# Two layers of block attention and a gated mixer on one core: preparation of the first row pair, pieces of w_out, weight reloads and the next attention's first units put in other places

## The chip, the core and the metric

The kernel runs on one core of a Trainium2 chip. The core has a matrix engine (PE, with its weight loads PEld), a vector engine (DVE), a scalar engine (ACT), GpSimd (POOL) and SyncE (SP), which here only issues transfers for 16 DMA engines. Each engine works through its own instructions strictly in order; semaphores tie them together. The metric is the device time of one execution in microseconds, lower being better. Before the change it is 2241.38 us, the median of three runs (2240.36 to 2242.91).

## What is computed

Two kinds of layer alternate, A B A B, on one sequence of 2048 rows of 640 elements, with one set of weights for both A and one for both B. Cut from the reference:

```
def _A_ref(x, wq, wk, wv, wo, beta):          # 32 heads of 20, 4 blocks of 512 rows
    q, k, v = (x @ wq), (x @ wk), (x @ wv)    # per head and block
    phi = lambda t: where(t > 0, t + 1.0, exp(t))
    for s in range(4):
        p = softmax(q_s k_s^T * scale + mask); a_dot = p v_s
        a_mem = (phi(q_s) M) / (phi(q_s) z + 1e-6)
        o = g * a_mem + (1 - g) * a_dot       # g = sigmoid(beta)
        M += phi(k_s)^T v_s; z += sum(phi(k_s))
    return o @ wo

def _B_ref(x, w_in, w_sp, b_sp, w_out):       # 2 * 864 columns
    z = gelu(x @ w_in); z1 = z[:, :864]; z2 = layernorm(z[:, 864:])
    g = w_sp @ z2 + b_sp[:, None]             # over the 2048 rows
    return (z1 * g) @ w_out

x = x + _A_ref(layernorm(x), ...); x = x + _B_ref(layernorm(x), ...)   # twice
```

## The kernel before, in words

Matrices are split into a high and a low half in f16 and multiplied in three products (hh, hl, lh), so a product that looks like 8 matmuls of the sequence is 24 on PE. Rows go in 16 tiles of 128.

The program runs in stages, each over the tiles of one layer: attention of layer 0 (60 to 593 us), the first half of its mixer (`phase1b`, to 795), the fold of its rows with w_sp, the gate and w_out (`phase2f`, to 1151), a lead in which PE already computes the first units of attention 1 (to 1211), attention 1 (to 1695), the mixer of layer 1 (`phase1b` again, to 1897) and its fold (`phase2s`, to the end).

`phase1b` goes over the tiles in the order 0 to 7, 12 to 15, 8 to 11. For each tile PE multiplies the split and transposed activations `th` with w_in in two halves of 30 matmuls (L384). `attn_out` (L352) makes the next tile's attention residual, `xn_t` (L371) its layer norm, its split (`xnhl`) and its transposing DMA into `th` (L309). `z2_half` and `z1_half` read the products out with a gelu. A tile's end is kept in `g.mark[i]`. Inside this stage a list scheduler puts the instructions of each engine in order, the earlier in the program the sooner; `high_priority` and `issue_after` bend that.

`phase2f` folds w_sp over pairs of row tiles, in the manner of Strassen: seven products P1 to P7 of 24 matmuls (L777) for each of eight pairs, over quarters of w_sp that are scaled, split (`hi`, `lo`: L741, L745), turned by a transposing DMA (`T`, L754, into `wt`), stored in `turned` for layer 1 (`st`, L757), copied back to f32 on POOL (`bk`, L762), mixed on DVE (`mS`, L765) and split once more (`H` on ACT, L768; `L` on DVE, L771). P2 needs H1 and L1, P3 H2 and L2. The results are put together on DVE (`v`, `q`, `u`, L784), gated with z1 (`gm`, L829, fetched from DRAM by L788), split (`gh`, `gl`), turned into `ut` (`gT`, L846), multiplied with w_out in a tail of 42 matmuls (`tl`, L854) and added to x (`ad`, L859). `SEVEN` (L695) lists these steps for one pair in the order in which every engine takes them; +n puts a step n pairs later, -n earlier. Steps of the first pair that lie ahead of its P1 form the list `ahead`; the first part of it, up to T12, is put behind the marks of mixer tiles 8 to 15 in equal distances, at high priority. From there on the order is by hand (`manual_schedule`). `staged` (L798) splits w_out into seven pieces (L90 on ACT, L91 on DVE) in `w0`: one behind each product of the first pair. In the last pair w_q, w_k and w_v are loaded back into `zb0`, `zb3` and `zb4` (L958) behind P1, P2 and P3; `turned()` (L1309) brings the normed rows of block 0 as `xt` behind P4 (L1307).

In the lead, `unit` (L1398) makes a tile of 128 columns of q or k for a block of 512 rows in 15 matmuls (L1409). ACT and DVE read it out and split it (L1429, L1433; for k also phi, L1432 to L1450, whose turned form is `pk`, L1452), SP stores it to `st` (L1525, L1526) and later loads it by heads as `qk` (L1539). Units a (q 0), b (k 0) and c (q 1) are written to psum banks of the fold; `kept_back` holds their readouts until the fold's memory is given back. Two tails (`finish`, L973) stand between the units. Then come eight value units (`value`, L1342; 15 matmuls each, L1353), and between them `unit(0, 1, only="k")`, which, called without `own`, makes q and k of tile 1 in new banks, q for the second time.

`phase2s` of layer 1 does the same fold with the quarters stored before: `bring` (L523) loads a stored quarter (L528) or turns one again (L530). `g.wu.load` brings w_out back in 14 loads (L162).

## Time and profile before

| what | value |
|---|---|
| median of three runs | 2241.38 us |
| the profiled execution's own time | 2243.77 us |
| its span, first to last instruction | 2242.0 us |
| mean granted clock of PE | 0.981 |
| attention 0, 60 to 593 us | PE busy 487.09 of 533.00 us, clock 0.97 |
| mixer 0, tiles up to 741.6 us | PE busy 148.12 of 148.60, clock 1.00 |
| fold 0, 854 to 1100 us | PE busy 245.76 of 246.18, DVE 220.59, clock 1.00 |
| attention 1, 1211 to 1695 us | PE busy 456.16 of 483.94, ACT 395.05, POOL 374.81 |
| mixer 1, 1695 to 1897 us | PE busy 201.35 of 202.13 |
| fold 1, from 1921 us | PE busy 315.47 of 321.00, DMA share 0.79 |

The profile is one execution, taken by the hardware profiler, a little slower than the median. The first rows are its whole, the others stretches of it with the busy time of the engines. A row of the timeline gives the start in microseconds, the busy time, the engine, the line, the operation, output and input, the count of equal instructions merged, and in brackets how long the engine had idled before the first of them and what ended that. PE's busy times are modelled from pipelined matmuls, so consecutive rows overlap by some 0.15 us: the distance between two starts is the safer measure. The stretches left out of the table are those that the change touches.

### The profile page before, as it was taken

Reading aid. Unit: us, or ns where it says so; the run is one execution under the profiler, and the core shown is the slowest. Engines: PE = TensorE matmul, PEld = TensorE weight load, DVE = VectorE, ACT = ScalarE, POOL = GpSimd, SP = SyncE. Lnnn points to the kernel's source line nnn. Section 1 sums busy time; section 2 is a strip of 40 time slices with the busy share of each in tenths; the row PEclk is TensorE's granted clock in tenths of the full one; section 3 lists DMA queues with packets and bytes.
Section 4 is the critical chain, followed back from the end, with each engine's and each line's share of the span. In section 5 each row is a group of like instructions: output and inputs, shape, how many; then the busy total and the mean of one; then the engine's idle time right before and its main releaser. Section 6 shows DMA issues by size and latency. Waiting matters only on the chain. (4 is left out here: it accounts for less than half of the span.)

```text
span 2242.0 us, 48924 instructions
## 1 busy us (share of the span) xinstructions
PE 2087.5 (93%) x19740; PEld 1255.8 (56%) x19740; DVE 1623.1 (72%) x2952; ACT 1219.6 (54%) x1491; POOL 1084.2 (48%) x704
## 2 busy tenths in 40 slices
PE   4888999999899888999898999999999999999999
PEld 2455665667555444555454556566665555555555
DVE  8678888787776789899644787877776667465455
ACT  3499888888542333323222898888874334223221
POOL 2398989888332422453330798788884223000000
PEclk9999999999999999999999999999999999999999
DMA  5626535356845667998764345343567334987975
GB/s 163 184 71 216 139 97 141 106 131 178 203 116 185 151 180 189 257 232 231 200 158 136 90 108 133 99 115 103 143 167 206 93 112 129 246 196 189 228 209 133
DMA packets 516340, 356.57 MB, mean 159 GB/s; under 512 B 410064, under 2 KB 452816, under 8 KB 510992
## 3 DMA queue, kind: packets, MB, share of 16 engines
q1 hardware_dynamic: 516112, 353.44, 59.8%
q8 instruction: 155, 2.54, 0.5%
q14 instruction: 73, 0.60, 0.1%
HBM read 157.44 MB, written 107.82 MB: 118 GB/s over the span
## 5 line engine op out<-in xcount | busy, mean ns | idle before, releaser
L1608 POOL TENSOR_TENSOR PHL<-P,PHL 128x1024 f16<-128x1024 f32 x310 | 658.9, 2133 | 204.4 <-ACT PHL L1607 158.2
L1589 ACT ACTIVATE P<-es,sc 128x1024 f32<-128x1024 f32 x320 | 356.2, 1113 | 92.7 <-PE es L1553 90.0
L1599 DVE TENSOR_REDUCE mx<-mp 128x2 f32<-128x1024 f32 (+2 forms) x384 | 321.1, 862 | 85.2 <-PE mp L1553 84.2
L1607 ACT CAST PHL<-P 128x1024 f16<-128x1024 f32 x320 | 333.5, 1042 | 6.3
L384 PEld LDWEIGHTS <-th 128*128 128x128 f16 x1920 | 188.0, 98 | 172.6 <-DMA th<-xnhl 9.6
L777 PEld LDWEIGHTS <-wt 128*128 128x128 f16 x1344 | 132.7, 99 | 142.3 <-DVE wt L771 17.0
L1642 PEld LDWEIGHTS <-PHL 128*128 128x128 f16 x5120 | 167.1, 96 | 56.8 <-DVE oat L1663 19.8
L537 PEld LDWEIGHTS <-wt 128*128 128x128 f16 x1344 | 131.4, 98 | 114.6 <-DMA wt<-wn 2.2
L1642 PE MATMUL pv<-vs,PHL 128*128 128x41 f16 x5120 | 172.7, 181 | 19.7 <-DVE oat L1663 16.5
L384 PE MATMUL zp<-wi,th 128*128 128x432 f16 x960 | 182.1, 348 | 8.0 <-DMA th<-xnhl 7.9
L295 POOL TENSOR_TENSOR lnrs<-lnve,mhalf 128x1 f32<-128x1 f32 x78 | 50.0, 649 | 288.1 <-DVE lnve L294 238.5
L384 PE MATMUL zp<-w,th 128*128 128x432 f16 x960 | 180.4, 346 | 0.7 <-ACT z L397 0.7
L762 POOL TENSOR_TENSOR f<-wt 128x1024 f32<-128x1024 f16 x32 | 82.4, 2577 | 171.1 <-DVE wt L771 124.9
L1409 PEld LDWEIGHTS <-zb 128*128 128x128 f16 x1215 | 105.0, 99 | 105.0 <-issue 9.5
L1582 PEld LDWEIGHTS <-qk 64*128 64x128 f16 (+1 forms) x1728 | 66.0, 94 | 125.6 <-issue 94.5
L1582 PE MATMUL mp<-qk 60*128 60x512 f16 (+3 forms) x864 | 108.5, 305 | 15.1 <-DVE mx L1599 9.7
L1385 PE MATMUL yps<-wo,o 128*128 128x320 f16 x720 | 122.3, 307 | 0.0
L1582 PE MATMUL es<-qk 64*128 64x256 f16 (+3 forms) x864 | 107.0, 300 | 10.1 <-ACT P L1589 7.3
L854 PE MATMUL cyp<-w,ut 128*128 128x320 f16 (+1 forms) x672 | 93.9, 299 | 1.6 <-DMA ut<-un 1.6
L1353 PE MATMUL vps<-zb,zb 128*128 128x320 f16 x480 | 76.8, 309 | 16.9 <-DVE qhl L1433 6.3
L589 DVE SCALAR_TENSOR_TENSOR xo<-cyp,xs,cx 128x640 f32<-128x640 f32 x14 | 12.4, 884 | 107.6 <-DMA out_dram<-xo 80.9
L1353 PE MATMUL vps<-zb,w 128*128 128x320 f16 x480 | 83.6, 306 | 4.4 <-DVE phl L1450 4.4
(299 smaller groups left out, 4238.0 us busy)
## 6 DMA issues: line engine op xcount, KB each, us to landing
wr<-in_B_w_sp_dram SPq DMA_DIRECT2D x32, 1024.0 KB
qk<-st SPq DMA_DIRECT2D x216, 120.0 KB
z<-z SPq DMA_DIRECT2D x32, 432.0 KB
cz<-z SPq DMA_DIRECT2D x32, 432.0 KB
turned<-wt SPq DMA_DIRECT2D x24, 512.0 KB
wt<-turned SPq DMA_DIRECT2D x24, 512.0 KB
st<-qhl SPq DMA_DIRECT2D x41, 256.0 KB
st<-khl SPq DMA_DIRECT2D x40, 256.0 KB
```

The lines of the kernel that those rows point to most:

```text
L384: nc.tensor.matmul(zp[:, n, :FHH], a[:, k, :], b[:, k, c:c + FHH], start=(k == 0 and j == 0), stop=(k == KD - 1 and j == 2))
L537: nc.tensor.matmul(o[:, :FHH], wt[:, x, m, :], zb[b][:, y, m, :], start=start and i == j == 0, stop=i == NP - 1 and j == 2, skip_group_che ...
L777: nc.tensor.matmul(o[:, :FHH], w[:, x, m, :], zb[b][:, y, m, :], start=start and i == j == 0, stop=i == NP - 1 and j == 2, skip_group_chec ...
L1353: nc.tensor.matmul(ps, a[:, k, c], b[:, k, n * 320:(n + 1) * 320], start=(i == 0), stop=(i == 14))
L1385: nc.tensor.matmul(ps, a[:, k, :], b[:, k, c], start=(i == 0), stop=(i == 14))
L1409: nc.tensor.matmul(ps, a[:, k, c], b[:, k, :], start=(i == 0), stop=(i == 14))
L1582: nc.tensor.matmul(out[:, h, o:o + w], a[r, ac], b[r, bc], start=o == 0, stop=False, skip_group_check=True)
L1589: self.last_of["ACT"] = nc.scalar.activation(self.Pf[t], es, AF.Exp, scale=g.esc).ins
L1599: self.last_of["DVE"] = nc.vector.tensor_reduce(mx[:, e, :, i], mp[:, :, o:o + w], AX.X, ALU.max).ins
L1607: nc.scalar.copy(hl[:, 0], P)
L1608: (nc.gpsimd if t < self.T - self.TAIL or t % 2 == 0 else nc.vector).tensor_tensor(hl[:, 1], P, hl[:, 0], ALU.subtract)
L1642: nc.tensor.matmul(pv[:, i, h, 0:PVC - 1], self.P[u][:, x, h, o:o + 128], v[:, j, h0 + h, :], start=first and h == x == 0 and (u, o, i, j) ...
```

## The change

1. `phase1b`: the loads of tile i + 2 are written ahead of tile i's products, and `xn_t` of tile i + 1 directly behind its `attn_out`, both ahead of `z2_half`. This holds for both layers.
2. `phase2f`: the first pair's preparation follows a table, `PREPARED`, which names for each step the mixer tile (1 to 14 in the order of the loop) behind which it stands. Only rows, T and sm or st keep the high priority. Ten steps at the end (H1 to hi22 of the second pair) have no tile and open the order by hand.
3. The pieces of w_out stand behind P1, P3, P4, P5, P6 and P7 of the first pair and P1 and P2 of the second.
4. w_q, w_k and w_v are loaded back behind P4, P5 and P6 of the last pair, `turned()` behind P5. Attention 1's `start` is issued behind the last gate's low half (`nxt.filled`).
5. The lead: three small places of the fold on the right side of memory (`fp`, `ftr1`, `ftr0`) are given back early, and `hl`, `tmp` and `pk` of the units get pools there (`epk`, `eu2`). Nothing is kept back: units a, b, c and d (k 1) are read out as they come, with a tail behind c and a tail behind d. The call in the middle of the values, and with it the second q of tile 1, is gone.

The rows below are orders of instructions as the two kernels have them; the line numbers of the changed kernel are 2 lower in `phase2s` and 5 to 10 higher from `phase2f` on. First SP's queue in the last pair of `phase2f`, before and then changed. The names: `turned` are stores of turned quarters, `zb` the reloaded weights, `cz` and `cx` fetches of z1 and x1, `ut` turned gates, the last transposes those of `turned()`.

```order
L757 DMA turned_1<-wt 128x2048 x2
L958 DMA zb_157<-w_q 128x6400
L788 DMA cz_15376<-z_0_12 128x864
L788 DMA cx_15384<-x_0_13 128x640
L846 DMA_TRANSPOSE ut<-un 128x14x128
L958 DMA zb_158<-w_k 128x6400
L928 DMA x_10<-cx_15267 128x640
L1302 DMA xn<-xnhl 128x1280
L958 DMA zb_159<-w_v 128x6400
L846 DMA_TRANSPOSE ut<-un 128x14x128
L1307 DMA_TRANSPOSE zb_160<-xn 128x10x128 x4
```

The changed kernel's queue from the same place:

```order
L763 DMA turned_1<-wt 128x2048 x2
L794 DMA cz_15375<-z_0_12 128x864
L794 DMA cx_15383<-x_0_13 128x640
L853 DMA_TRANSPOSE ut<-un 128x14x128
L935 DMA x_10<-cx_15267 128x640
L1307 DMA xn<-xnhl 128x1280
L853 DMA_TRANSPOSE ut<-un 128x14x128
L968 DMA zb_157<-w_q 128x6400
L794 DMA cz_15605<-z_0_15 128x864
L968 DMA zb_158<-w_k 128x6400
L1312 DMA_TRANSPOSE zb_160<-xn 128x10x128 x4
```

The fetches of z1 and x1 and both transposes of `ut` moved ahead of the copies; that of w_v comes three rows further down, behind the transposes of `turned()`.

Next DVE in the lead, before: `cx<-cyp` adds a tail's result, `a`, `b`, `c` are the psum banks of the units, `qps` and `kps` those of the second call.

```order
L859 SCALAR_TENSOR_TENSOR cx_15722<-cyp,xs,cx_15722 128x640
L859 SCALAR_TENSOR_TENSOR cx_15759<-cyp,xs,cx_15759 128x640
L1433 SCALAR_TENSOR_TENSOR qhl<-a,qhl 128x512
L1433 SCALAR_TENSOR_TENSOR khl<-b,khl 128x512
L1438 TENSOR_SCALAR b<-b,sc 128x512
L1440 SCALAR_TENSOR_TENSOR b<-eq,sc,b 128x512
L1450 SCALAR_TENSOR_TENSOR phl<-b,sc,phl 128x512
L1433 SCALAR_TENSOR_TENSOR qhl<-c,qhl 128x512
L1359 SCALAR_TENSOR_TENSOR vs<-vps,vs 128x16x20 x2
L1433 SCALAR_TENSOR_TENSOR qhl<-qps,qhl 128x512
L1433 SCALAR_TENSOR_TENSOR khl<-kps,khl 128x512
```

The same stretch of DVE in the changed kernel, up to the values:

```order
L1438 SCALAR_TENSOR_TENSOR qhl<-a,qhl 128x512
L1438 SCALAR_TENSOR_TENSOR khl<-b,khl 128x512
L1443 TENSOR_SCALAR b<-b,sc 128x512
L1445 SCALAR_TENSOR_TENSOR b<-eq,sc,b 128x512
L1455 SCALAR_TENSOR_TENSOR phl<-b,sc,phl 128x512
L1438 SCALAR_TENSOR_TENSOR qhl<-c,qhl 128x512
L866 SCALAR_TENSOR_TENSOR cx_15722<-cyp,xs,cx_15722 128x640
L1438 SCALAR_TENSOR_TENSOR khl<-d,khl 128x512
L1443 TENSOR_SCALAR d<-d,sc 128x512
L1445 SCALAR_TENSOR_TENSOR d<-eq,sc,d 128x512
L1455 SCALAR_TENSOR_TENSOR phl<-d,sc,phl 128x512
L866 SCALAR_TENSOR_TENSOR cx_15759<-cyp,xs,cx_15759 128x640
```

The readouts of a, b and c moved ahead of both additions of the tails; the readout of d replaces that of qps and kps, and the eight readouts of values follow in one piece.

Last SP's queue at the end of layer 1's mixer, before: `th` are turned activations, `x` and `z` loads and stores of the mixer, `wt` the quarters for `phase2s`, `w` pieces of w_out.

```order
L530 DMA_TRANSPOSE wt<-wn 128x16x128
L309 DMA_TRANSPOSE th<-xnhl 128x10x128
L343 DMA x_27398<-x_1_11 128x640
L398 DMA z_1_8<-z_27326 128x864
L309 DMA_TRANSPOSE th<-xnhl 128x10x128
L398 DMA z_1_9<-z_27436 128x864
L309 DMA_TRANSPOSE th<-xnhl 128x10x128
L398 DMA z_1_10<-z_27534 128x864
L528 DMA wt<-turned_1 128x2048
L530 DMA_TRANSPOSE wt<-wn 128x16x128
L162 DMA w_153<-w_uh 128x640
```

And the changed kernel's, from the same activations on:

```order
L309 DMA_TRANSPOSE th<-xnhl 128x10x128
L343 DMA x_27315<-x_1_11 128x640
L398 DMA z_1_8<-z_27312 128x864
L309 DMA_TRANSPOSE th<-xnhl 128x10x128
L398 DMA z_1_9<-z_27422 128x864
L309 DMA_TRANSPOSE th<-xnhl 128x10x128
L398 DMA z_1_10<-z_27520 128x864
L526 DMA wt<-turned_1 128x2048
L526 DMA wt<-turned_0 128x2048
L528 DMA_TRANSPOSE wt<-wn 128x16x128 x2
L398 DMA z_1_11<-z_27613 128x864
L162 DMA w_153<-w_uh 128x640
```

The first transpose of a quarter and the load of a turned quarter, which stood some tiles earlier, moved behind the last but one store of z, next to the other two.

The diff, cut to its core:

```diff
         for i, t in enumerate(ts):
             late = lambda: ExitStack() if i else after(0)
+            b = load(ts[i + 2]) if i + 2 < NT else None
             if i + 1 < NT:
                 with late():
-                    xn = attn_out(ts[i + 1], *a)
+                    th1 = xn_t(attn_out(ts[i + 1], *a))
+            a = b
             last = z2_half(t, w_in_half(1, *th))
             g.mark[i] = last
-            if i + 2 < NT:
-                a = load(ts[i + 2])
-            with late():
-                th1 = xn_t(xn) if i + 1 < NT else None
...
+PREPARED = """
+rows1.0:1 rows0.0:1 max1.0:2 max0.0:4 sm0.0:4 sm1.0:4 hi11.0:5 lo11.0:6 hi22.0:7 lo22.0:8 T11.0:10 T22.0:10 hi21.0:10
+lo21.0:10 bk22.0:10 hi12.0:11 T21.0:11 rows1.1:11 st11.0:11 lo12.0:12 rows0.1:12 bk11.0:12 max1.1:12 st22.0:12 bk21.0:12
+mS1.0:14 mS3.0:14 max0.1:14 H1.0 L1.0 T12.0 mS2.0 sm1.1 sm0.1 hi11.1 st12.0 lo11.1 hi22.1
+""".split()
...
-    def behind(k):
+    def behind(k, n):
         held = ExitStack()
-        held.enter_context(tc.high_priority(offset=HP))
+        if n[0] in "rTs":
+            held.enter_context(tc.high_priority(offset=HP))
...
-    ahead = [(n, w - lag) for w in (-2, -1) for n, lag in order if w - lag >= 0]
-    cut = ahead.index(("T12", 0))
-    for i, (n, k) in enumerate(ahead[:cut]):
-        with behind(min(8 + 8 * i // cut + (n[0] in "Ts"), 15)):
-            item(n, k)
+    ahead = []
+    for w in PREPARED:
+        (n, k), _, m = (w.partition(":")[0].split("."), *w.partition(":")[1:])
+        if m:
+            with behind(int(m), n):
+                item(n, int(k))
+        else:
+            ahead.append((n, int(k)))
...
-            if n[0] == "P" and w == 0:
+            if (w, n) in ((0, "P1"), (0, "P3"), (0, "P4"), (0, "P5"), (0, "P6"), (0, "P7"), (1, "P1"), (1, "P2")):
                 next(wu, None)
-            if w + 1 == NP and n in ("P1", "P2", "P3"):
-                a = "qkv"[int(n[1]) - 1]
+            if w + 1 == NP and n in ("P4", "P5", "P6"):
+                a = "qkv"[int(n[1]) - 4]
                 nc.sync.dma_start(g.wf[a], g.wkept[a])
-            if w + 1 == NP and n == "P4":
-                nxt.turned()
-        if w == 0:
-            for _ in wu:
-                pass
+                if n == "P5":
+                    nxt.turned()
...
     run = lambda it: [None for _ in it]
-    nxt.kept_back = []
-    for nm, m, o in (("q", 0, "a"), ("k", 0, "b"), ("q", 1, "c")):
+    slots.close()
+    nxt.pk = side(nxt.late, "epk", 2)
+    early = ExitStack()
+    nxt.u2 = side(early, "eu2", 3)
+    for nm, m, o in (("q", 0, "a"), ("k", 0, "b"), ("q", 1, "c"), ("k", 1, "d")):
         run(nxt.unit(0, m, {nm: bank(o)}))
-        if (nm, m) != ("q", 0):
+        if m:
             finish(pend.pop(0))
+    early.close()
...
-    todo, nxt.kept_back = nxt.kept_back, None
-    for f_ in todo:
-        f_()
     pb_.close()
     nxt.psum()
     with tc.manual_schedule(engines=ALLE):
         for t in range(4):
             run(nxt.value(t))
-            if t == 0:
-                run(nxt.unit(0, 1, only="k"))
```

24 lines of the change are left out of this document (14 added, 10 removed).

## The prediction, written before the changed kernel was run

> **What bounds the kernel now.** I read the page first, for the engines' shares of the span. Then I read the busy time by stage (the windows view), for the stages in which the busiest engine pauses. Last I read the timeline of each engine there, for what it paused on. In the windows the columns are the stretch, its length, then the busy time and count of PE, of its weight loads, of DVE, ACT and POOL, the granted clock, the DMA share and GB/s.
>
> ```profile
> PE 2087.5 (93%) x19740; PEld 1255.8 (56%) x19740; DVE 1623.1 (72%) x2952; ACT 1219.6 (54%) x1491; POOL 1084.2 (48%) x704
> 741.60:795.06 53.46, 46.05 (x243) 23.83 (x240) 35.98 (x53) 20.04 (x30) 25.40 (x21) 0.97 0.58 153
> 795.06:849.62 54.56, 37.78 (x196) 19.08 (x194) 48.83 (x65) 20.38 (x25) 14.07 (x7) 0.89 0.72 196
> 1100.18:1151.44 51.26, 44.48 (x253) 25.09 (x252) 21.38 (x39) 10.16 (x13) 11.68 (x10) 0.93 0.79 211
> 1151.44:1211.06 59.62, 48.74 (x281) 28.62 (x280) 20.89 (x41) 14.23 (x23) 6.21 (x9) 0.91 0.54 143
> 1897.13:1921.00 23.87, 22.10 (x122) 11.69 (x121) 9.21 (x10) 9.93 (x11) 2.96 (x4) 1.00 1.02 268
> ```
>
> PE sets the time: it is busy for 93% of the span. So a microsecond is won only where PE pauses, or where it does work that goes away. The first four stretches are where this change reaches PE: the last mixer tiles of layer 0, the first pair of its fold, its last pair, and the lead into the second attention. PE idles there for 7.4, 16.8, 6.8 and 10.9 us, 41.9 in all, and the clock is below 1.00 in each. The fifth is the start of layer 1's fold, where PE hardly idles but the DMA engines are full (share 1.02).
>
> **Part 1: the first pair's preparation goes to earlier tiles.** Rows of PE, then of POOL and DVE; the bracket is the idle time ahead and what ended it.
>
> ```profile
> 748.01 5.63 PE L384 MATMUL zp<-w,th 128*128 128x432 f16 x30 [0.71 <-ACT z L397]
> 757.51 7.33 PE L384 MATMUL zp<-wi,th 128*128 128x432 f16 x30 [3.86 <-DMA th<-xnhl]
> 773.15 5.65 PE L384 MATMUL zp<-wi,th 128*128 128x432 f16 x30 [2.83 <-DMA th<-xnhl]
> 743.76 2.12 POOL L762 TENSOR_TENSOR f<-wt 128x1024 f32<-128x1024 f16 x1 [12.14 <-DMA wt<-wn]
> 746.42 0.73 DVE L301 TENSOR_SCALAR z<-z,lnmv,lnrs 128x864 f32<-128x864 f32 x1 [6.68 <-POOL lnrs L295]
> ```
>
> POOL stood 12.14 us at the copy back (L762) of a turned quarter that had not landed. The layer norm's root (L295), queued behind it, came late, DVE waited 6.68 for that, and the split activations reached PE late. In the order of after, T11 and T22 issue some two tiles earlier and POOL's copies come later, when these quarters have landed. So the three waits go: 7.40, and with them 1.69 of low clock (30 matmuls took 7.33 after the 3.86 wait, 5.64 otherwise): 9.1. What is late next: SP now has the store of T11 (st11) ahead of the transposed load th of a following tile, and a store of a quarter can't issue before the quarter has landed. T11 itself issues behind the large stores that keep w_in. The trace shows no such pairing. From below it costs nothing; from above about what went, 9.1. The nearest row is the wait of 3.86, a th held up by the landing of such a quarter, so I take 3.6, one wait of nearly that size without its clock. **Gain 5.5, from 0 to 9.1.**
>
> **Part 2: the fold's first pair and the start of the second.**
>
> ```profile
> 795.06 4.54 PE L777 MATMUL a<-zb,wt 128*128 128x432 f16 x24
> 805.88 0.90 PE L777 MATMUL c<-zb,wt 128*128 128x432 f16 x2 [6.28 <-ACT wt L768]
> 812.61 4.54 PE L777 MATMUL b<-zb,wt 128*128 128x432 f16 x24
> 816.99 4.54 PE L777 MATMUL a<-zb,wt 128*128 128x432 f16 x24
> 841.96 0.53 PE L777 MATMUL c<-zb,wt 128*128 128x432 f16 x2 [2.14 <-DVE u L784]
> 849.62 6.43 PE L777 MATMUL c<-zb,wt 128*128 128x432 f16 x22 [7.13 <-DVE wt L771]
> ```
>
> A product of 24 matmuls takes 4.38 from start to start (812.61 to 816.99). The second product waited 6.28 for H1, which now is made before the mixer ends; so is L1. Three products then take 13.1, not the 21.9 from 795.06 to 816.99. But the gain does not reach the end of the second pair's start whole. That pair's second product needs L1 of its own rows. The chain to it starts with a transposed quarter that reuses a tile of the first pair and waits for the third product to end; before, 32.6 passed from there to the product's resumption at 849.62. DVE is busy for 48.83 of these 54.56, and its work behind the third product stays, but for one piece of w_out, that is about 0.9. So the resumption comes 13.1 + 31.7 = 44.9 behind the fold's start, where it was 54.56. The waits of 2.14 and 7.13 do not go: they become one of about 9.4, with the low clock behind it as before (eight products need only 35.0). **Gain 9.7.** If the chain shrinks by the DVE work that left with the pieces and the rows (some 3 more), 12.5; if the pieces moved into the second pair fall on the chain too, 7. The later pairs' order is unchanged.
>
> **Part 3: the last pair.** Rows of PE, of DVE, and of SP, which issues the transfers.
>
> ```profile
> 1116.22 6.25 PE L777 MATMUL b<-zb,wt 128*128 128x432 f16 x22 [6.75 <-DVE wt L771]
> 1122.31 2.88 PE L854 MATMUL cyp<-w,ut 128*128 128x320 f16 x20
> 1113.97 1.06 DVE L829 TENSOR_TENSOR u<-u,cz 128x864 f32<-128x864 f32 x1 [9.75 <-DMA cz<-z]
> 1104.75 0.32 SPq L958 DMA_DIRECT2D zb<-w_q  x1
> 1105.12 0.43 SPq L788 DMA_DIRECT2D cz<-z  x1
> 1089.71 0.98 SPq L757 DMA_DIRECT2D turned<-wt  x2
> ```
>
> The third product waited 6.75 for L2, which DVE made only after a gate (L829) that waited 9.75 for its z1. SP had that fetch behind w_q's copy, and w_q's copy behind the first product. In after, the fetch stands right behind the stores at 1089.71, about 14 us ahead of its use, and the copies come later. The wait goes, and with it the low clock: 22 matmuls ran 6.09 from 1116.22 to 1122.31, where 22/24 of 4.38 is 4.02. **Gain 6.75 + 2.07 = 8.8**; 6.7 if some of it returns. The three copies of 1600 KB and the four transposes into xt now share the 29 us from the third product's end to the first unit (two tails and four products). At the 211 GB/s of this stretch's window a copy takes some 7.8 us; the first unit needs two of them and the transposes, and the third copy is wanted only by the value units, 30 us later. So I cost them at nothing; if the third copy holds the transposes up, its 7.8 bound the cost.
>
> **Part 4: the lead.**
>
> ```profile
> 1151.44 3.40 PE L1409 MATMUL a<-zb,zb 128*128 128x512 f16 x15
> 1154.68 3.40 PE L1409 MATMUL b<-zb,zb 128*128 128x512 f16 x15
> 1159.69 5.88 PE L854 MATMUL cyp<-w,ut 128*128 128x320 f16 x42 [1.60 <-DMA ut<-un]
> 1165.40 3.40 PE L1409 MATMUL c<-zb,zb 128*128 128x512 f16 x15
> 1176.14 2.20 PE L1353 MATMUL vps<-zb,zb 128*128 128x320 f16 x15 [1.63 <-DVE qhl L1433]
> 1183.02 4.16 PE L1353 MATMUL vps<-zb,zb 128*128 128x320 f16 x15 [4.68 <-DVE qhl L1433]
> 1186.97 4.26 PE L1409 MATMUL qps<-zb,zb 128*128 128x512 f16 x15
> 1199.47 11.74 PE L1353 MATMUL vps<-zb,zb 128*128 128x320 f16 x75 [2.97 <-DVE phl L1450]
> 1164.79 0.72 ACT L1294 CAST xnhl<-xt 128x640 f16<-128x640 f32 x1 [4.03 <-POOL xt L1290]
> 1167.81 0.69 ACT L1432 ACTIVATE eq<-b,sc 128x512 f32<-128x512 f32 x1
> 1195.71 0.69 DVE L1433 SCALAR_TENSOR_TENSOR khl<-kps,khl 128x512 f16<-128x512 f32 x1 [3.12 <-ACT eq L1432]
> 1198.67 0.75 DVE L1450 SCALAR_TENSOR_TENSOR phl<-kps,sc,phl 128x512 f16<-128x512 f32 x1 [0.81 <-ACT phl L1449]
> 1174.61 0.88 DVE L859 SCALAR_TENSOR_TENSOR cx<-cyp,xs,cx 128x640 f32<-128x640 f32 x1 [8.06 <-PE cyp L854]
> 1207.66 0.49 DVE L1359 SCALAR_TENSOR_TENSOR vs<-vps,vs 128x320 f16<-128x320 f32 x1 [1.54 <-ACT vs L1358]
> ```
>
> From the last product's end (1151.44, call it E) to the end of the eight value units the lead takes 59.6: the 75 matmuls start at 1199.47 and, at 11.6 of net time, end at 1211.06. In after PE has a, b, c in a row, then a tail, d, a tail, eight value units; the qps unit at 1186.97 (q of block 1 a second time) is gone, 15 matmuls. A unit takes 3.24 (1151.44 to 1154.68) and a tail 5.71 (1159.69 to 1165.40), so without waits d ends at E + 4 x 3.24 + 5.71 = E + 18.7; the first tail's ut came 8.3 behind E and is needed at 9.7. The second tail writes the psum tile that L859 of the first must have read, and in DVE's new order L859 stands behind the readouts of a, b and c. These start when ACT has done the last xnhl cast (1164.79, E + 13.4) and run on ACT to the end of eq (1168.50, E + 17.1); from khl to the end of phl takes DVE 3.7 (1195.71 to 1199.42), then come qhl of c (0.69) and L859 (0.88). So L859 ends at E + 22.3 and the second tail waits 3.6, with some 1.9 of low clock behind it, as after the 4.68 wait (15 matmuls in 4.16, not 2.20). It ends at E + 29.9, and eight value units at the 2.03 that they take one after another (0.49 + 1.54) at E + 46.2. **Gain 59.6 - 46.2 = 13.4.** Without that wait it is 18.9; with waits of the value units for the readout of d besides, 9.
>
> A rule of the Trainium skill bears on such waits: "TensorE: Matmul & The Clock Gate", section "What's actually happening", has the clock fall to half after an idle window of about 3.4 us. The rows agree for 3.86 and 4.68, and not quite at 2.97, after which 75 matmuls took 1.4 more than five units at 2.03. By that rule a wait of 3.6 is on the edge: if no whole window is idle the sum is 1.9 lower.
>
> **Part 5: layer 1.** The mixer's new order of issue moves transfers there as well.
>
> ```profile
> 1858.34 1.82 SPq L530 DMA_TRANSPOSE wt<-wn  x1
> 1892.22 3.49 SPq L530 DMA_TRANSPOSE wt<-wn  x1
> 1916.58 4.55 PE L537 MATMUL gb<-zb,wt 128*128 128x432 f16 x24 [1.77 <-DMA wt<-wn]
> ```
>
> The transpose at 1858.34 and the load of the first turned quarter now stand beside the one at 1892.22, ahead of w_out's loads and of the quarter that the fifth product waits for, in the stretch where the DMA share is 1.02. That is one more of 3.49 and one more issue of 0.32, so all behind it is 3.8 later and the wait of 1.77 becomes 5.6, long enough for the 1.7 of clock. **Loss 5.5**; nothing if the queue makes it up, 8 if the second product waits too. By the Trainium skill, "DMA: Bandwidth & Descriptors", section "Latency and other measured facts", a transpose runs at 261 GB/s; 512 KB would be an estimated 2.0 us, and the loss about 4. No row here times one alone.
>
> **Sum.** -5.5 - 9.7 - 8.8 - 13.4 + 5.5 = -31.9, against the profiled execution's 2243.77 (its span of 2242.0 and 1.8 around it): 2211.9. The runs' median of 2241.38 is 2.4 lower, so 2209.5.
>
> **Rivals.**
> 1. *Waits only move* (chance 0.15): the tile behind st11 waits for all of the 9.1, and the second pair's start keeps its distance. Parts 1 and 2 give nothing: -8.8 - 13.4 + 5.5 = -16.7, 2224.7. For it: DVE's 48.83 of 54.56.
> 2. *Fewer new waits* (0.17): layer 1's queue makes up its delay and the second tail does not wait: 5.5 and 5.5 better, 2198.5. For it: the 1.77 wait is one alone in 24 us.
> 3. *The lead does not do what it says* (0.08): with own places and early readouts the value units still wait for DVE, and only the doubled unit goes (4.26, or 4.1 net): 9.3 worse, 2218.8. Against: nothing in the new order but the readout of d is between them.
> 4. *Slower than before* (0.05): layer 1's fold never makes up the late transfers, and the fifth product of each of its eight pairs waits 3.8 with 1.7 of clock. That is 8 x 5.5 = 44 in place of 5.5: 2248.0. It decides from seven pairs on (the other parts give 37.4). Against it: its DMA share falls behind the first pair, since PE waits little there.
>
> **How the numbers follow.** The forecast has 0.55. The range takes in rivals 1 to 3 with their bounds: below, 9.1 for part 1 and rival 2 (2195); above, rival 1 with part 4 somewhat short (2227). Slower is rival 4; an interval of 0.2% (4.5 us), what a measurement can tell here from no change, needs part 4 to fail on top of rival 1: 0.03. Faster keeps 0.92.
>
> **What would show it.** Part 1: no wait of PE for th over 3 us but one, in the tile behind st11. Part 2: one wait of 9 to 10 at the second product of the second pair, some 45 behind the fold's start. Part 3: no wait in the last pair. Part 4: one wait of 3 to 4 ahead of the second tail, and 46 from E to the end of the values. Part 5: the wait at the fifth product of layer 1 at 5 to 6. The prediction is wrong if turned xt or a copy of w_q, w_k or w_v ends a wait of the first unit, or if PE waits in the second to seventh pair.

## The result, and the profile after

| | before | after |
|---|---|---|
| median | 2241.24 us (4 runs, 2240.36 to 2242.91) | 2215.26 us (4 runs, 2211.22 to 2218.62) |
| profiled execution | 2243.77 us, span 2242.0 | 2214.95 us, span 2213.2 |
| mean granted clock of PE | 0.981 | 0.984 |

The ratio of the times is 0.9882 with a 95% interval of 0.9865 to 0.9900: faster by 26 us. The four runs of the changed kernel lie further apart (7.4 us) than these four of before (2.6), but in later sets of nine the kernel before lay 8.1 and 9.2 us apart too.

Below, the page's busy times and then the windows view of the changed kernel, whose columns are as in the prediction: mixer 0, the start of fold 0, the last 51.26 us of its products (with the last pair in them), the lead, and the first five products of fold 1.

```profile
PE 2077.6 (94%) x19725; PEld 1253.1 (57%) x19725; DVE 1623.4 (73%) x2951; ACT 1218.7 (55%) x1490; POOL 1082.9 (49%) x704
595.03:795.07 200.04, 194.08 (x1085) 106.16 (x1082) 145.34 (x264) 72.10 (x103) 69.74 (x64) 0.98 0.62 167
795.07:841.29 46.22, 36.05 (x195) 18.87 (x194) 43.38 (x54) 19.33 (x25) 14.11 (x9) 0.93 0.75 213
1082.64:1133.90 51.26, 51.26 (x304) 29.54 (x302) 26.35 (x45) 11.29 (x15) 10.59 (x9) 1.00 0.77 240
1133.90:1179.70 45.80, 42.11 (x265) 26.32 (x264) 20.29 (x40) 14.17 (x24) 9.97 (x11) 0.96 0.71 178
1864.07:1890.96 26.89, 23.76 (x120) 12.17 (x121) 8.83 (x10) 9.75 (x11) 2.58 (x4) 0.94 1.12 266
```

The last pair is full (51.26 of 51.26 busy, clock 1.00), the lead idles 3.7 instead of 10.9, the fold's start still 10.2. The mixer still idles 6.0, and layer 1 now has a share of 1.12 on the DMA engines and a clock under 1. Cut at PE's first matmul of each stage, the two spans compare as follows (us; the resumption is that of the second product of the second pair, E the last product's end, and the lead runs to the unit behind the values):

| stretch | before | after | difference | predicted |
|---|---|---|---|---|
| start to mixer 0 | 593.31 | 595.03 | +1.7 | 0 |
| mixer 0 | 201.75 | 200.04 | -1.7 | -5.5 |
| fold 0, start to resumption | 54.56 | 46.22 | -8.3 | -9.7 |
| resumption to E | 301.82 | 292.61 | -9.2 | -8.8 |
| lead | 59.62 | 45.80 | -13.8 | -13.4 |
| attention 1 and mixer 1 | 686.07 | 684.37 | -1.7 | 0 |
| fold 1, first five products | 23.84 | 26.89 | +3.05 | +5.5 |
| the rest | 321.03 | 322.24 | +1.2 | 0 |
| span | 2242.0 | 2213.2 | -28.8 | -31.9 |

The start to mixer 0, which the change does not touch, lay between 590.8 and 596.7 in the runs below. Runs of one kernel in one set differed by up to 11 us, and those of the kernel before over all sets by 12.6 (2235.72 to 2248.32). So I judge the experiments by such stretches, most of which repeat: six kernels with the changed kernel's code there (itself among them) gave 198.4 to 200.0 for mixer 0, seven gave 46.2 to 46.4 for the resumption, and seven 45.8 to 46.0 for the lead. Two stretches repeat less well. Mixer 0 in the code of before took 201.75, 201.84 and once 204.86. In fold 1 the first five products took 21.9 to 23.8 in the two kernels with the old code and the old memory, 24.8 to 27.9 in those with the changed one, and the rest of that fold 318.4 to 324.9 whatever the code.

**Mixer 0 after:** rows of PE, of SP (the stores `w_i0h`, `w_i0l` keep w_in's second half, 1080 KB each) and of DVE, which makes the input `xnhl` of the late `th`.

```profile
618.43 5.65 PE L384 MATMUL zp<-wi,th 128*128 128x432 f16 x30 [1.34 <-DMA th<-xnhl]
738.07 7.88 PE L384 MATMUL zp<-wi,th 128*128 128x432 f16 x30 [4.62 <-DMA th<-xnhl]
720.13 0.42 SPq L190 DMA_DIRECT2D w_i0h<-w  x1
720.60 0.64 SPq L190 DMA_DIRECT2D w_i0l<-w  x1
722.53 8.74 SPq L760 DMA_TRANSPOSE wt<-wn  x2
731.37 0.89 SPq L763 DMA_DIRECT2D turned<-wt  x1
732.83 2.13 SPq L309 DMA_TRANSPOSE th<-xnhl  x1
726.85 0.82 DVE L308 TENSOR_TENSOR xnhl<-xt,xnhl 128x640 f16<-128x640 f32 x1 [0.79 <-ACT xnhl L307]
```

The three old waits are gone and one of 4.62 is there, with 2.25 of low clock (7.88, not 5.65). Its `th` had its input at 727.67, but SP was busy for 8.74 with issuing two transposes of quarters, directly behind the stores of w_in, and came to it at 732.83.

**Fold 0 after** (products are L783 now, DVE's results L790): PE, then DVE, ACT and POOL around the wait.

```profile
833.63 0.52 PE L783 MATMUL c<-zb,wt 128*128 128x432 f16 x2 [2.13 <-DVE u L790]
841.29 6.02 PE L783 MATMUL c<-zb,wt 128*128 128x432 f16 x22 [7.14 <-DVE wt L777]
817.59 2.73 DVE L91 SCALAR_TENSOR_TENSOR w<-wst,iv,w 128x640 f16<-128x640 f32 x1
832.11 0.89 DVE L91 SCALAR_TENSOR_TENSOR w<-wst,iv,w 128x640 f16<-128x640 f32 x1 [1.92 <-ACT w L90]
824.88 0.83 ACT L90 ACTIVATE w<-wst,iv 128x640 f16<-128x640 f32 x1 [9.88 <-DMA wst<-in_B_w_out_dram]
816.79 2.85 POOL L768 TENSOR_TENSOR f<-wt 128x1024 f32<-128x1024 f16 x1 [1.40 <-DMA wt<-wn]
```

The first pair runs without a wait over 0.6, but the waits ahead of the second pair's second product stand as before, 2.13 and 7.14. DVE is busy for 43.38 of 46.22; ACT waited 9.88 for a piece of w_out (`wst`). DVE's first addition behind the third product (`q`) and the piece that runs beside a POOL addition stand so in the kernel before (first two rows) and in the changed one (third row; its piece is the L91 at 817.59 above):

```profile
821.43 0.65 DVE L784 SCALAR_TENSOR_TENSOR q<-b,unt,v 128x432 f32<-128x432 f32 x1
825.92 2.74 DVE L91 SCALAR_TENSOR_TENSOR w<-wst,iv,w 128x640 f16<-128x640 f32 x1
813.12 0.65 DVE L790 SCALAR_TENSOR_TENSOR q<-b,unt,v 128x432 f32<-128x432 f32 x1
```

From `q` to the resumption it is 28.19 before (to 849.62) and 28.17 after (to 841.29): DVE works off the same list, with four pieces of w_out in it both times.

**The lead and layer 1 after:** PE, DVE (the addition of the first tail), then SP and PE at the fifth product of fold 1.

```profile
1156.41 7.15 PE L861 MATMUL cyp<-w,ut 128*128 128x320 f16 x42 [3.69 <-DVE cx L866]
1155.48 0.88 DVE L866 SCALAR_TENSOR_TENSOR cx<-cyp,xs,cx 128x640 f32<-128x640 f32 x1
1859.24 7.39 SPq L528 DMA_TRANSPOSE wt<-wn  x2
1884.89 6.24 PE L535 MATMUL gb<-zb,wt 128*128 128x432 f16 x24 [3.12 <-DMA wt<-wn]
```

The first tail's addition ends at 1156.36, 22.5 behind E (1133.90), and the second tail waits 3.69 for it. In layer 1 the fifth product waits 3.12 instead of 1.77 and then runs at a lower clock (6.24, not 4.55).

### The profile page after: what moved, and what is told of

It reads as the page before. It is cut to its first block, busy times and chain, and to the rows that moved or that the text cites. A ratio compares the mean times of both kernels' runs of the same rounds, so it can differ in the third digit from the quotient of the medians.

```text
span 2213.2 us, 48872 instructions
## 1 busy us (share of the span) xinstructions
PE 2077.6 (94%) x19725; PEld 1253.1 (57%) x19725; DVE 1623.4 (73%) x2951; ACT 1218.7 (55%) x1490; POOL 1082.9 (49%) x704
## 4 chain that ended last, share of the span: by engine, by line
PE 65%; DVE 11%; ACT 8%; DMA 7%; issue 4%; POOL 2%; SPq 2%; ACTq 0%; DVEq 0%; POOLq 0%
PE zp L384 14%; PE cyp L861 3%; PE cyp L584 3%; PE vps L1358 3%; PE pv L1647 3%; PE yps L1390 3%; ACT P L1594 3%; PE qps L1414 3%; PE mp L1587 3%; PE gb L535 3%; PE b L783 3%; PE ga L535 2%; PE a L783 2%; PE kps L1414 2%; ACT PHL L1612 2%
## 5 line engine op out<-in xcount | busy, mean ns | idle before, releaser
L783 PEld LDWEIGHTS <-wt 128*128 128x128 f16 x1344 | 131.8, 98 | 125.8 <-DVE wt L777 8.8
L1601 DVE TENSOR_REDUCE mx<-mp 128x4 f32<-128x1024 f32 x64 | 77.7, 1215 | 11.5 <-PE mp L1558 11.4
```

What stands on the lines that cost most here:

```text
L783: nc.tensor.matmul(o[:, :FHH], w[:, x, m, :], zb[b][:, y, m, :], start=start and i == j == 0, stop=i == NP - 1 and j == 2, skip_group_chec ...
```

## The experiments

All but two are edits of the changed kernel; those two start from the kernel before.

### Mixer 0: what holds the th up

**The stores of quarters without high priority.**

```diff
-        if n[0] in "rTs":
+        if n[0] in "rT" or n[:2] == "sm":
```

> The changed kernel with the stores of the first pair's turned quarters (st11, st22) no longer at high priority, so the first of them stands behind the x1 store and the th that it held up before; everything else as in the changed kernel. Theory of the prediction (the store, waiting for T11's landing ahead of th, made the wait of 4.62 us at th in the 12th mixer tile): the wait falls below 1 us, its low clock of 2.25 goes, and the mixer (first zp of the mixer to the fold's first product, 200.0 us now) is 6 to 7 us shorter. Rival (the two transposes T11 and T22 themselves hold SP, 8.74 us of issue behind the 2160 KB that keep w_in): the store costs SP 0.89 us at most, the wait stays above 3 us and the mixer is at most 1.5 us shorter.

PE's rows of this run:

```profile
734.70 5.65 PE L384 MATMUL zp<-wi,th 128*128 128x432 f16 x30 [3.31 <-DMA th<-xnhl]
748.84 7.33 PE L384 MATMUL zp<-wi,th 128*128 128x432 f16 x30 [3.02 <-DMA th<-xnhl]
```

The wait falls from 4.62 only to 3.31, and a second one of 3.02 comes at a later `th`; mixer 0 takes 201.0, no less than before the edit. So the prediction's theory (the store of T11 ahead of `th`) falls as the main cause: the edit took 1.3 from the wait, and the transposes held SP for 8.61 here too.

**w_in's second half kept three tiles later.**

```diff
-                if first and i in (7, 9):
+                if first and i in (7, 12):
```

> The changed kernel with the two 1080 KB stores that keep the second half of w_in put behind the 13th mixer tile, not the 10th, so T11 and T22 no longer stand behind them in SP's queue; st11 and now also st22 still stand ahead of the th. Theory of the prediction (st11 waits for the landing of T11): T11 still has to land, so the wait at th stays at 2 to 5 us. Rival (T11 and T22 were slow to issue because the queue was full of the stores): their issue falls from 8.74 to about 4 us, T11 lands some 4 to 5 us earlier, the wait of 4.62 falls below 1 and the mixer is 6 to 7 us shorter, unless the stores hold up a later th (then a new wait stands behind the 13th tile).

SP and PE of this run:

```profile
720.65 4.52 SPq L760 DMA_TRANSPOSE wt<-wn  x2
771.15 7.33 PE L384 MATMUL zp<-wi,th 128*128 128x432 f16 x30 [4.47 <-DMA th<-xnhl]
```

Without the 2160 KB ahead of them the same two transposes issue in 4.52 instead of 8.74, and the wait in that tile falls to 1.32. But the stores (issued from 757.14 to 758.46 here) then hold up the `th` that is issued at 760.71 (4.47): 200.4, no gain. Moved there, the stores only move the wait.

**w_in's second half kept one tile earlier,** where no transposed quarter follows closely.

```diff
-                if first and i in (7, 9):
+                if first and i in (7, 8):
```

> The changed kernel with the two 1080 KB stores that keep the second half of w_in put one mixer tile earlier, so they have run when T11 and T22 issue. Theory (the stores fill the queue, whatever stands behind them waits): T11 and T22 issue in 4 to 6 us together in place of 8.74, the wait of 4.62 at the 12th tile falls to 1.5 or less, and the mixer takes 193 to 196 us from its first product to the fold's first, not 199.1 to 200.0; about 4 to 6 us faster in all. Rival (the two transposes are slow by themselves and hold th up whatever is ahead of them, or the stores hold up the th of the tile at which they now stand): a wait of 3 us or more stays in one of the tiles 10 to 13, and the mixer is at most 2 us shorter.

SP and PE of this run:

```profile
717.52 4.98 SPq L760 DMA_TRANSPOSE wt<-wn  x2
730.63 5.65 PE L384 MATMUL zp<-wi,th 128*128 128x432 f16 x30 [1.87 <-DMA th<-xnhl]
```

Of the waits for `th` over 0.6 one of 1.87 with no loss of clock is left; mixer 0 takes 194.8, 5.3 less than in the changed kernel, and the one run took 2205.42. With the run before it this settles the place: the backlog of the stores of w_in, met by the moved transposes.

### Fold 0: what sets the resumption

**Without the maxima of row tiles 4 and 5** (constants in their place, so the third pair is scaled otherwise).

```diff
-                nc.vector.tensor_reduce(am, raw[t], AX.X, ALU.max, apply_absolute_value=True)
+                if t in (4, 5):
+                    nc.vector.memset(am, 2.0 ** -10)
+                else:
+                    nc.vector.tensor_reduce(am, raw[t], AX.X, ALU.max, apply_absolute_value=True)
```

> The changed kernel without the maxima of the two row tiles of the third pair (tiles 4 and 5; a constant takes their place, so their scale is another one): DVE has two reductions of 2.27 us less between the fold's third product and the second product of the second pair, all else is the same. Theory of the prediction (DVE's list of work sets that resumption, 46.2 us behind the fold's start): it comes 4 to 4.6 us earlier, at 41.6 to 42.2, and the wait of 7.14 ahead of it is about 2.6 to 3.1. Rival (the landing of a turned quarter, which waits for the third product, sets it, and DVE only looks busy): the resumption stays within 1 us of 46.2.

ACT, DVE and PE of this run:

```profile
825.65 0.83 ACT L90 ACTIVATE w<-wst,iv 128x640 f16<-128x640 f32 x1 [9.84 <-DMA wst<-in_B_w_out_dram]
826.51 0.89 DVE L91 SCALAR_TENSOR_TENSOR w<-wst,iv,w 128x640 f16<-128x640 f32 x1 [2.97 <-ACT w L90]
841.60 7.00 PE L783 MATMUL c<-zb,wt 128*128 128x432 f16 x22 [7.13 <-DVE wt L777]
```

4.5 of DVE's work is gone and the resumption moves by 0.3 (45.94). By itself that speaks against DVE's list. But the rows show where the time went: DVE now idles 2.97 for ACT, which waits for a piece of w_out. A second bound may stand right behind the first, and the next two runs test that.

**Each piece of w_out loaded one piece earlier,** into the second of the two buffers that exist already.

```diff
-        for k in range(w.nk):
+        def load(k):
...
             nc.sync.dma_start(st, w.dram[k * 128:k * 128 + n])
+            return n, st
+
+        nx = load(0)
+        for k in range(w.nk):
+            n, st = nx
+            nx = load(k + 1) if k + 1 < w.nk else None
             yield
```

> Where the second product of the second pair resumes in layer 0's fold (46.2 behind the fold's start in the changed kernel). The load of each piece of w_out is issued one piece earlier, so that its two buffers are both filled; nothing else differs. Theory A (VectorE's list of work is the chain, and the loads of the pieces come next behind it): ScalarE's wait of 9.88 for a piece goes, but the resumption stays at 45.5 to 46.2, since VectorE was busy up to 1.9 of its time. Theory B (the loads of the pieces alone set it): 42 to 44. Theory C (neither, a turned quarter or POOL's copies): 46.

**The same, and without the two maxima.**

> As the kernel with the loads one piece earlier, and the maxima of row tiles 4 and 5 are left out besides (a constant stands in their place, so the third pair is scaled otherwise). VectorE has 4.5 less to do and no late piece to wait for. Theory A (both bounds stand one behind the other): the resumption comes at 41 to 43 behind the fold's start, where leaving the maxima out alone gave 45.9. Theory C (a turned quarter or POOL's copies set it): it stays at 45.5 to 46.

PE's row of the first, then of the second:

```profile
836.72 5.84 PE L783 MATMUL c<-zb,wt 128*128 128x432 f16 x22 [7.13 <-DVE wt L777]
835.29 6.50 PE L783 MATMUL c<-zb,wt 128*128 128x432 f16 x22 [5.18 <-DVE wt L777]
```

With the loads alone ACT's wait of 9.88 goes and the resumption stays at 46.46. With both it comes at 42.03 (835.29 behind the fold's start at 793.26), a little over 4 earlier. Either alone gives at most 0.3. So DVE's list sets the resumption and the loads of the pieces come close behind it, which fits the 28.2 from `q` on in the kernels before and after.

### The last pair: order or bytes

**The copies where they were, the fetches ahead of w_q's.**

```diff
-            if w + 1 == NP and n in ("P4", "P5", "P6"):
-                a = "qkv"[int(n[1]) - 4]
+            if w + 1 == NP and n in ("fx1", "P2", "P3"):
+                a = {"fx1": "q", "P2": "k", "P3": "v"}[n]
                 nc.sync.dma_start(g.wf[a], g.wkept[a])
-                if n == "P5":
-                    nxt.turned()
+            if w + 1 == NP and n == "P4":
+                nxt.turned()
```

> The changed kernel with w_q, w_k and w_v loaded back at the early places of before (behind P1, P2, P3 of the last pair), except that w_q's copy stands behind the fetches of z1 and x1, not ahead of them; the transposes of ut stand behind w_q's copy, as before the change. Theory of the prediction (the wait of 6.75 us in the last pair came from z1's fetch standing in SP's queue behind w_q's copy, which waited for P1): no product of the last pair waits, and from the pair's first product to its last product's end it takes 42.1 us as in the changed kernel. Rival (the 1600 KB themselves were the trouble, whatever stands behind them): ut or another transfer comes late, and the last pair has a wait of 2 us or more again.

SP's transposes of `ut` in the changed kernel (first two rows) and in this run (next two), then PE of this run:

```profile
1095.64 1.29 SPq L853 DMA_TRANSPOSE ut<-un  x1
1102.89 1.72 SPq L853 DMA_TRANSPOSE ut<-un  x1
1094.84 4.04 SPq L853 DMA_TRANSPOSE ut<-un  x1
1105.65 6.32 SPq L853 DMA_TRANSPOSE ut<-un  x1
1116.59 7.54 PE L861 MATMUL cyp<-w,ut 128*128 128x320 f16 x42 [2.93 <-DMA ut<-un]
1159.31 5.87 PE L861 MATMUL cyp<-w,ut 128*128 128x320 f16 x42 [3.38 <-DVE cx L866]
```

The theory's 42.1 is missed: from the pair's first product to the last product's end it takes 47.3, and the rival's sign is there. `ut`, now behind the copies, takes 4.04 and 6.32 to issue and a tail waits 2.93 with 1.7 of clock. From the fold's start to E it is 5.1 more (343.96, not 338.83); the lead gives 1.6 of that back (44.21), since the second tail's wait of 3.38 cost no clock here. At the third product no wait is left, so for that wait the place of z1's fetch was what mattered. The run does not separate two reasons why that fetch was late before: SP stood from 1090.7 to 1104.75 for w_q's copy, and the fetch, issued at 1105.12 behind that copy's 1600 KB, let the gate start only at 1113.97. Both go when it stands ahead. So the order frees the third product, and that the copies come later is what keeps `ut` in time.

### The lead

**The kernel before, with the doubled q unit left out.**

```diff
-                run(nxt.unit(0, 1, only="k"))
+                run(nxt.unit(0, 1, {"k": nxt.bank(0, 1, "k")}))
```

> The kernel before the change with one edit: the call in the middle of the values makes only k of tile 1, so q of tile 1 is no longer made a second time (15 matmuls, two readouts and two stores less). Theory of the prediction (the doubled unit is worth its 4.1 us of PE and nothing more; the other 9 to 10 us of the lead's gain are waits that the early readouts take away): from the last product's end to the end of the values 55.0 to 56.5 us in place of 59.6, and the waits of 1.63, 4.68 and 2.97 ahead of value units are still there. Rival (the doubled unit's readout on ACT and DVE was what the value units waited for, so most of the gain is its): 50 us or less.

One of its waits, in a row of PE:

```profile
1185.01 4.16 PE L1353 MATMUL vps<-zb,zb 128*128 128x320 f16 x15 [4.35 <-DVE qhl L1433]
```

The lead takes 55.98, 3.6 less than before, and its waits stay (1.63, 4.35, 2.97). So the doubled unit is 3.6 of the 13.8, and if the parts add, the other 10.2 come from the order and the own places. (The one run took 2239.10, no less than the run of the kernel before beside it, 2237.08: single runs cannot show 3.6.)

**The readouts of a, b and c held back behind the first tail.**

```diff
-    for nm, m, o in (("q", 0, "a"), ("k", 0, "b"), ("q", 1, "c"), ("k", 1, "d")):
+    outs = []
+    nxt.out = lambda *a: outs.append(a)
+    for nm, m, o in (("q", 0, "a"), ("k", 0, "b"), ("q", 1, "c")):
         run(nxt.unit(0, m, {nm: bank(o)}))
-        if m:
-            finish(pend.pop(0))
+    del nxt.out
+    t = pend.pop(0)
+    tail(t)
+    nxt.out(*outs[0])
+    summed(t)
...
+    nxt.out(*outs[1])
+    nxt.out(*outs[2])
+    run(nxt.unit(0, 1, {"k": bank("d")}))
+    finish(pend.pop(0))
```

> The changed kernel with the readouts of units a, b and c held back until the first tail is issued, so that on DVE the addition of that tail (L866) stands behind the readout of a and ahead of those of b and c; PE's order is the same. Theory (the second tail waits 3.69 us only for this addition, which stands behind the chain of ACT and DVE over b and c): the addition ends about 1 us behind the first tail, ahead of unit d's end, the wait goes, its low clock (second tail 6.99 us from start to start, not 5.70) goes too, and from the last product's end to the end of the values it takes 40 to 41.5 us in place of 45.8: 4.5 to 5.5 us faster. Rival (the readouts of b, c and d now come later and the value units wait for them, since their psum banks are the same): the wait moves to the value units, and the lead is at most 2 us shorter.

PE of this run, the second tail and the values:

```profile
1151.01 5.87 PE L861 MATMUL cyp<-w,ut 128*128 128x320 f16 x42
1156.72 4.24 PE L1368 MATMUL vps<-zb,zb 128*128 128x320 f16 x30
1161.36 12.38 PE L1368 MATMUL vps<-zb,zb 128*128 128x320 f16 x90 [0.40 <-DVE vs L1374]
```

The wait ahead of the second tail is gone, and its clock loss with it; the lead takes 41.23, 4.6 less. The wait was DVE's order, as the prediction had it.

### Layer 1: what moved the transposes

**The kernel before, with 4 KB per partition held from the lead to the end of mixer 1** by a tile that nothing uses, as the changed kernel's `epk` does.

```diff
     sb.close()
     rest.close()
+    nxt.late = ExitStack()
+    nxt.late.enter_context(tc.tile_pool(name="epk", bufs=1, side="right")).tile([128, 1024], F32, name="epk")
     nxt.sbuf()
...
         if i:
+            att[1].late.close()
             phase2s(g, w_sp, x1_d[i], z1_d, zb, xs[i + 1])
```

> The kernel before the change with one edit: an unused tile of 4 KB per partition is held on the right side of memory from the lead to the end of layer 1's mixer, where the changed kernel holds the two pk tiles of its lead. No work is added; the mixer's buffers of layer 1 stand 4 KB further along. Theory now (the pk tiles, not the mixer's new order, moved the transposes: the quarters for layer 1's fold then overlap mixer buffers that are in use to the end): the two transposes of quarters issue together behind the last but one store of z, as in the changed kernel, and the wait at the fold's fifth product grows from 1.77 to 2.8 to 3.2 us; from the first product to the sixth 24.9 to 26.9 us in place of 23.8. Theory of the prediction (the mixer's new order moved them): nothing changes, 1.77 and 23.8.

SP and PE of this run:

```profile
1895.85 0.80 SPq L528 DMA_DIRECT2D wt<-turned  x2
1896.70 6.89 SPq L530 DMA_TRANSPOSE wt<-wn  x2
1922.82 7.38 PE L537 MATMUL gb<-zb,wt 128*128 128x432 f16 x24 [3.68 <-DMA wt<-wn]
```

The order of the mixer's code is that of before, and still SP issues two loads and two transposes side by side as in the changed kernel. The fifth product waits 3.68 and the five products take 28.6, not 23.8; that is more than expected, since 2.8 of clock went as well. So the held memory alone is enough to move the transposes. Whether the new order of the mixer alone would do it too was not tried. The size is less sure than the cause. The run with the doubled q unit left out, whose mixer is the old one, has its transposes at the old places and no wait at all at the fifth product:

```profile
1913.59 4.54 PE L537 MATMUL gb<-zb,wt 128*128 128x432 f16 x24
```

### Together

**w_in kept at tile index 8 and the lead's readouts behind the first tail.**

> The changed kernel with both improvements together: w_in's second half is kept one tile earlier (tile index 8, not 9), and the lead's units a, b and c are read out behind the first tail. If the two places are independent, their gains add: 5.3 in layer 0's mixer (194 to 195.5 from its first zp to the fold) and 4.6 in the lead (41.2 from E to the unit behind the values), so the profiled run comes at about 2215 - 9.9 = 2205 and the time is 0.983 to 0.985 of the kernel before. If the earlier stores only move the wait into a place that the other edit opens, one of the two distances goes back to what it was in the changed kernel (200 or 45.8).

Median of five runs 2204.63 us (2201.92 to 2205.93), 0.9831 of before, interval 0.9817 to 0.9844, which lies below that of the changed kernel (0.9865 to 0.9900). PE's row in mixer 0:

```profile
731.99 7.33 PE L384 MATMUL zp<-wi,th 128*128 128x432 f16 x30 [2.72 <-DMA th<-xnhl]
```

The lead takes 41.6, mixer 0 196.5: a wait of 2.72 that here cost clock as well, so 1 over the expected 195.5. Between the medians it is 10.6, with 9.9 expected.

**The same, with the loads one piece earlier and three of the second pair's sums on GpSimd.**

```diff
...
             mix(*{"1": ("f2", "f1", "f2", ALU.add), "3": ("f1", "f0", "f1", ALU.subtract),
-                  "2": ("f0", "f2", "f0", ALU.subtract), "4": ("f1", "f1", "f0", ALU.subtract)}[b])
+                  "2": ("f0", "f2", "f0", ALU.subtract), "4": ("f1", "f1", "f0", ALU.subtract)}[b],
+                eng=nc.gpsimd if k == 1 and b != "4" else nc.vector)
```

> All gains in one kernel: w_in's second half kept at tile index 8, the lead's units read out behind the first tail, each piece of w_out loaded one piece earlier, and the three sums of the second pair's quarters (mS1, mS3, mS2; 1.13 each from start to start on VectorE) made by GpSimd, which stood idle for some 31 us there. If VectorE's list of work sets the resumption of layer 0's fold (theory A), taking 3.4 from it brings the resumption from 46.4 behind the fold's start to 42.5 to 43.5, with mixer and lead as before (194 to 197, 41.6), and the time to some 2201, 0.981 to 0.983 of the kernel before. If the pieces of work on the other engines set it, it stays at 46 and the time at 2204 to 2205. If the sums on GpSimd come late or slow VectorE beside them, it is over 46.5.

POOL, DVE and PE of this run:

```profile
813.70 7.69 POOL L771 TENSOR_TENSOR f<-f,f 128x1024 f32<-128x1024 f32 x3
817.40 2.29 DVE L884 TENSOR_REDUCE am<-wr 128x1 f32<-128x2048 f32 x1 [0.90 <-DMA wr<-in_B_w_sp_dram]
819.61 2.47 DVE L91 SCALAR_TENSOR_TENSOR w<-wst,iv,w 128x640 f16<-128x640 f32 x1
834.45 7.09 PE L783 MATMUL c<-zb,wt 128*128 128x432 f16 x22 [7.13 <-DVE wt L777]
```

A miss: the resumption comes at 45.45, one earlier than in the kernel that it builds on (46.44), not three to four. Of the 3.4 that left DVE, 0.9 went into a wait for rows of w_sp and 1.6 into one instruction: this L91 took 2.47 beside POOL's sums, 0.88 without. The median of five runs is 2206.07 us (2199.24 to 2210.42), 0.9832 with an interval of 0.9813 to 0.9851: no difference that these runs can tell from the kernel with two gains (0.9817 to 0.9844). The simpler one is the better of the two.

## Why the prediction was right, and where not

The time, 2209.5 against 2215.26, lay in the range and on the right side, 5.8 too low. Of that, 2.7 is the choice of runs: the profiled execution, from which the sum starts, was 2.4 above the median that the sum used before, and 0.3 below the median after. Parts 3 and 4 held, part 2 held in size; the largest error is that of the mixer. That the five parts together came to -30.0, so near the -31.9, is in part luck: the mixer gave 3.8 less than put, and layer 1 cost 2.45 less than put.

**Part 1 (-5.5, measured -1.7): wrong in the size of what comes next, and in its cause.** That the three waits and their clock would go, 9.1, was right. The failing step is "The nearest row is the wait of 3.86 ... so I take 3.6, one wait of nearly that size without its clock", put behind the store of T11. The wait came as 4.62 with 2.25 of clock, 6.9 instead of 3.6. (The third tile's wait was 0.86 longer besides, but that is scatter: 0 to 0.29 in the five other kernels with this mixer.) The sign, one wait over 3 in the tile behind st11, came true by another cause than the one named. That cause was in the sentence ahead, which I passed over: T11 issues behind the large stores that keep w_in. Taking the store's priority away did not shorten the mixer (201.0); keeping w_in a tile earlier brought it to 194.8, which is 7.0 below before.

**Part 2 (-9.7, measured -8.3): right in size and in the limit, wrong in the picture of the waits.** The rule "DVE is busy for 48.83 of these 54.56, and its work behind the third product stays" held, and the run without maxima and with early loads shows it: only with DVE's work and the pieces' loads both eased did the resumption move (42.03). "They become one of about 9.4" did not happen: 2.13 and 7.14 remained two, 9.27 together. The forecast of 44.9 was 1.3 short: behind the third product's end (808.21, its start at 803.83 and 4.38) the rest took 33.1, not the 31.7 that I had from 32.6 less one piece of w_out. That piece is the term that failed: none left this part of DVE's list. From `q` on, four pieces stand in it before and after, and it takes 28.2 both times; the other 0.5 was lost ahead of `q`.

**Part 3 (-8.8, measured -9.2 with 0.4 of clock behind the resumption): right.** No wait in the last pair, no copy that held up a first unit. The run with the early copies shows both halves of it: with the fetch ahead the third product does not wait, and the later copies keep `ut` in time. That the copies would hold up `ut` where they stood was not in the prediction.

**Part 4 (-13.4, measured -13.8): right, step by step.** The addition of the first tail was put at E + 22.3 and ended at 22.5; the wait was put at 3.6 and was 3.69; the second tail took 6.99 from start to start, 5.71 and 1.28 of clock where I took 1.9 (1.3 to 1.7 in six other runs, nothing in one). That the order on DVE makes the wait is shown by the run that takes it away.

**Part 5 (+5.5, measured +3.05): right in sign and place, too large, and with a cause that is not needed.** The step that failed is "The mixer's new order of issue moves transfers there as well": holding as much memory as the units' `pk` did it in a kernel with the old order; whether the new order has any part is open. That the transposes move stood in SP's order, so the sign did not hang on this cause. The size was "all behind it is 3.8 later", taken one to one as a wait. SP's issue of the transpose that the fifth product waits for, before and after:

```profile
1905.24 7.77 SPq L530 DMA_TRANSPOSE wt<-wn  x1
1875.28 7.44 SPq L528 DMA_TRANSPOSE wt<-wn  x1
```

Counted from the fold's start it began 3.1 later (11.21, not 8.11), but the product's wait grew by 1.35 only, and the clock took 1.69 as put. By the scatter of the other runs (21.9 to 23.8 with the old code, 24.8 to 27.9 with the changed one) the loss lies between 0.9 and 6.0. The rest of fold 1 was 1.2 longer, which is within its scatter.

Of the rivals, the one in which waits only move was half true in the mixer alone; that fewer waits would follow, and that the lead would not do what it says, were not seen; the later pairs of fold 1 did not wait 3.8 each (the rest of the fold was 1.2 longer in all).

## What to carry to other kernels

A transfer that is issued earlier has to be placed against the bytes that stand ahead of it in the queue: read the backlog of large stores at the new place, since a short transposing load behind it inherits the wait. When an engine is busy for nine tenths of a stage (43.38 of 46.22 here), easing it alone may show nothing because a second bound stands close behind; take both away together before the first is called innocent. Memory that an early stage holds can put a later stage's prefetches at other places (28.6 for five products instead of 23.8 in the run with the held tile), so a new buffer is a term of the sum too.

## What the hardware showed that I had not expected

**Waits of about 3 us cost clock or not.** At the fifth product of fold 1 waits of 2.68 to 3.10 cost nothing in four runs (4.55 for the product), waits of 3.12 to 4.12 cost 1.7 in seven (6.24), and one of 3.68 cost 2.8 (7.38, the run with the held memory). But in mixer 0 waits of 2.72 and 3.02 cost 1.7 and one of 3.31 nothing (7.33, 7.33 and 5.65 for 30 matmuls). Ahead of the second tail a wait of 3.38 cost 1.67 in one run (7.54, w_in three tiles later) and nothing in another (5.87, the early copies). The length of the wait alone does not decide it. The Trainium skill, "TensorE: Matmul & The Clock Gate", section "What's actually happening", has an idle window of about 3.4 us that is free-running. That it is free-running would fit the scatter; a loss behind a wait of 2.72, shorter than one such window, does not fit the figure.

**The issue of a transposing DMA grows with what stands ahead of it.** Two equal transposes took SP 8.74 and 8.61 right behind 2160 KB of stores, 4.98 and 4.52 where the stores stood elsewhere; a transpose of `ut` took 1.29 or 1.72, and 4.04 or 6.32 behind the copies of 1600 KB. In that time SP issues nothing else. The stores are not all of it: in the kernel before the two took 7.18 at 736.71, with the stores issued 18 us ahead (718.05).

**POOL's elementwise work holds up some of DVE's.** The piece's low half (L91, two operands in SBUF) took 0.88 alone and 2.73 and 2.47 where a POOL addition ran, ending 0.7 behind POOL's end each time (816.79 and 2.85, 813.70 and 7.69). In the kernel before it took 2.74 at the same place, so the change has no part in it. Other instructions of DVE with two such operands do the same in the changed kernel: the low half of a quarter (L751) took 3.14 at 808.91 instead of 1.27, and L777 took 2.08 at 814.39 instead of 1.21, each ending 1.1 behind POOL's end. The maximum of a row tile, with one operand, took its 2.3 beside POOL's sums too. The Trainium skill, "GPSIMD Engine Reference", section "1. Specifications", names contention of the two engines where a DVE instruction has two SBUF inputs; these rows agree, and it took 1.6 of the 3.4 that the last experiment meant to win.
